# Four heads at a time: batching the heads of a gated linear attention in front of a cosine-gated MLP

## The chip, the cores and the metric

One NeuronCore of a Trainium2 chip runs the whole program. The time is what the device needs for one execution, in microseconds (us). Four timed runs of the kernel before gave 470.71 to 471.46 us with a median of 471.32. The profiled execution took 471.46 us.

The engines are named as in the profile: PE is TensorE's matmul, PEld its weight load, DVE is VectorE, ACT is ScalarE, POOL is GpSimd, SP is SyncE, which here only issues DMAs.

## The reference

The inputs q, k, v and f_logit have the shape (batch 4, heads 8, sequence 768, head size 48). For each batch and head a 48 x 48 state runs along the sequence; its rows decay by a gate, and the query reads it:

```python
f = 1.0 / (1.0 + np.exp(-f_logit))
for t in range(S):
    state = f[:, :, t, :, None] * state + np.einsum('bhd,bhe->bhde', k[:, :, t], v[:, :, t])
    y[:, :, t] = np.einsum('bhd,bhde->bhe', q[:, :, t], state)
```

The heads are then put side by side to a matrix x of 3072 tokens by 384, and an MLP with a cosine gate follows:

```python
h = x @ w_in            # 384 -> 2048
g = h * np.cos(h)
return g @ w_out        # 2048 -> 384
```

## The kernel before, in words

The program is written in a tile language: the code allocates tiles from pools, each tag (the tile's name) with its number of buffers, and a planner puts the instructions of each engine in one fixed order and adds the semaphores. Operations of `nc.any` go to VectorE or ScalarE as the planner chooses. Each engine runs its own list in order; a waiting instruction holds up those behind it. All DMAs are issued by SP, in one list.

**Constants (L38 to L54).** An identity, an upper triangular mask `umask` (128 x 128), and both weight matrices, which are loaded first (6 MB) and cast to bfloat16 on VectorE.

**Preparation of a head (L62 to L116).** For each of the 4 batches, `attn_batch` loops over the 8 heads. The sequence is cut into 6 chunks of 128 tokens; a tile has the 128 tokens of a chunk on its partitions and chunk by head size, 6 x 48 = 288 columns. Four DMAs of 144 KB bring q, k, v and f_logit. GpSimd casts v (`vc`). ScalarE takes Sigmoid and Ln of f_logit (L77, L79); the product of `umask` with the logarithms gives their running sum within each chunk (`pCum`), and two exponentials of it (L84, L86) give the decay `b_td` and its inverse. Six small matmuls give the sum over each whole chunk (`pBC`, L90), and `bC` (L93) is its exponential, the decay of the state over a chunk. Sigmoid, Ln and Exp each need a table in ScalarE; a change of table is an ACT_TABLE_LOAD in the profile. GpSimd zeroes `QK_td` and writes q times decay and k times inverse decay into it (L96 to L100). TensorE transposes it chunk by chunk (`pQK`, L104), and two copies bring `Qb_dt` and `Kb_dt` back to SBUF (L107, L109).

**Recurrence (L117 to L141).** Chunk by chunk, and within a chunk head by head, one unit of work is done:

- `pA` (L121) is the 128 x 128 product of keys and queries in the chunk; `Am` (L124) is pA times the mask.
- `pS` (L127) is the chunk's own contribution to the state.
- `pY` adds two matmuls: `vc` with `Am` (L130) and the state before the chunk with the queries (L131). `Yt` (L133) is its bfloat16 copy, and a DMA of 12 KB writes it to `xT` in DRAM (L135).
- `stmp` (L138) is pS plus the old state, and the new state (L140) is stmp times the decay of the chunk.

There are 4 x 6 x 8 = 192 units. `vc`, `bC`, `QK_td`, `Qb_dt` and `Kb_dt` have 9 buffers each; the other tiles of the preparation have 3, and those of the recurrence 6. In PSUM pCum, pBC, pS and pY have one buffer each, pQK and pA two.

**MoE stage (L143 to L164).** Six blocks of 512 tokens read `xT` back, multiply by w_in, take the cosine gate (ScalarE's Sin, VectorE's product) and multiply by w_out. It is not touched.

Of the kernel before, what the change touches and what calls it, by code (L numbers as in the profile page):

```python
# [9 lines left out]
F32 = mybir.dt.float32  # L10
BF16 = mybir.dt.bfloat16
AF = mybir.ActivationFunctionType
# [4 lines left out]
def kernel(  # L17
# [10 lines left out]
    nc = tc.nc  # L28
    B, H, S, D = q.shape
    C = 128  # L30
    NCH = S // C
# [9 lines left out]
    make_upper_triangular(nc, umask, val=1.0, diag=True)  # L41
    halfpi = cpool.tile([128, 1], F32, name="halfpi")
# [18 lines left out]

    def attn_batch(b, sb, sb2, stpool, ps, ps2):  # L62
        vc_l, bC_l, Qb_dt_l, Kb_dt_l, Kb_td_l, state_l = [], [], [], [], [], []
        for h in range(H):
            qh = sb.tile([C, NCH, D], F32, name="qh")
            kh = sb.tile([C, NCH, D], F32, name="kh")
            vh = sb.tile([C, NCH, D], F32, name="vh")
            fh = sb.tile([C, NCH, D], F32, name="fh")
# [3 lines left out]
            nc.sync.dma_start(out=fh, in_=f_logit[b, h].rearrange("(c p) d -> p c d", p=C))  # L72
            vc = sb.tile([C, NCH, D], BF16, name="vc", bufs=9)
            nc.gpsimd.tensor_copy(out=vc, in_=vh)

            sigf = sb.tile([C, NCH, D], F32, name="sigf")
            nc.scalar.activation(out=sigf, in_=fh, func=AF.Sigmoid)  # L77
            logf = sb.tile([C, NCH, D], BF16, name="logf")
            nc.scalar.activation(out=logf, in_=sigf, func=AF.Ln)  # L79
# [8 lines left out]
            pBC = ps.tile([D, NCH], F32, name="pBC", tag="pBC")  # L88
            for c in range(NCH):
                nc.tensor.matmul(pBC[:, c:c + 1], lhsT=logf[:, c, :],  # L90
                                 rhs=umask[:, C - 1:C], start=(c == 0), stop=(c == NCH - 1))
            bC = sb.tile([D, NCH], F32, name="bC", bufs=9)
            nc.scalar.activation(out=bC, in_=pBC, func=AF.Exp, scale=1.0)  # L93

            QK_td = sb.tile([C, NCH, C], BF16, name="QK_td", bufs=9)
# [10 lines left out]
            Qb_dt = sb.tile([D, NCH, C], BF16, name="Qb_dt", bufs=9)  # L106
            nc.any.tensor_copy(out=Qb_dt, in_=pQK[0:D])  # L107
            Kb_dt = sb.tile([D, NCH, C], BF16, name="Kb_dt", bufs=9)
            nc.any.tensor_copy(out=Kb_dt, in_=pQK[64:64 + D])  # L109

            state = stpool.tile([D, D], BF16, name="state")
            nc.gpsimd.memset(state, 0.0)
            vc_l.append(vc); bC_l.append(bC)
            Qb_dt_l.append(Qb_dt); Kb_dt_l.append(Kb_dt)
            Kb_td_l.append(Kb_td); state_l.append(state)
        for c in range(NCH):  # L116
            for h in range(H):  # L117
# [88 lines left out]
```

## Time and profile before

| | |
|---|---|
| median of 4 runs | 471.32 us |
| profiled execution | 471.46 us |
| its span (first to last instruction) | 469.7 us |
| busy in the span: PE / DVE / ACT / POOL | 337.8 / 229.3 / 314.7 / 85.0 us |
| DMA queue q1, share of 16 engines' span | 33.6% |
| attention, to the end of the last Yt | 333.7 us |
| MoE stage, from its first matmul to the end | 131.0 us |

Busy time of an engine is the time in which one of its instructions ran. Matmuls are pipelined, so their ends overlap with the next ones and a busy PE is not PE at its peak. In a row of the timeline the first number is the start in us from the span's start, the second the time in us; the brackets give the idle time of that engine just before, and what ended it. In a row of a group of instructions the shapes are partitions x elements, and after the bar stand busy time in us and the mean of one in ns, then idle time before.

### The profile page before, as it was taken

The page shows a single profiled execution, that of the slowest core. Times are in us where ns is not written, and L with a number is a line of the kernel's source. Part 1 is how long each engine was busy: PE and PEld are TensorE (multiplying, and loading weights), DVE is VectorE, ACT ScalarE, POOL GpSimd, SP SyncE. Part 2 cuts the span into 40 slices and gives each one's busy share as a digit, 9 for nine tenths or more (in the row PEclk, how much of TensorE's full clock was granted, in tenths as well). Part 3 has the DMA queues.
Part 4 walks back from the last instruction along what each step waited for, and adds up shares of the span by engine and source line. Part 5 has one row for each costly group of instructions (what it writes and reads, how often), then busy time and mean ns, then how long its engine had stood idle before and what let it go on. Part 6 is the DMA issues. An engine that isn't in the chain of part 4 may idle for free.

```text
span 469.7 us, 6528 instructions
## 1 busy us (share of the span) xinstructions
PE 337.8 (72%) x1850; PEld 175.6 (37%) x1856; DVE 229.3 (49%) x704; ACT 314.7 (67%) x606; POOL 85.0 (18%) x168
## 2 busy tenths in 40 slices
PE   0024448797769973344778876998399999999997
PEld 0012224344434431222434443443145455554544
DVE  0413336675535551233556563555073847557381
ACT  1099998988955665999999786555191825537180
POOL 6133221046210060322201723000000000000000
PEclk9999999999999999999999999999999999999999
DMA  8995563121521116955411224000302110100101
GB/s 326 296 153 117 101 114 64 36 49 34 97 47 27 26 36 108 147 107 105 82 34 39 47 48 83 13 14 13 113 29 85 50 69 17 51 34 35 52 17 67
DMA packets 120996, 35.04 MB, mean 75 GB/s; under 512 B 113152, under 2 KB 120576, under 8 KB 120576
## 3 DMA queue, kind: packets, MB, share of 16 engines
q1 hardware_dynamic: 120960, 34.63, 33.6%
q8 instruction: 14, 0.23, 0.2%
q14 instruction: 22, 0.18, 0.1%
HBM read 27.53 MB, written 7.08 MB: 74 GB/s over the span
## 4 chain that ended last, share of the span: by engine, by line
PE 53%; issue 14%; ACT 14%; DMA 6%; SPq 5%; POOL 4%; DVE 3%; ACTq 0%; DVEq 0%; POOLq 0%
PE ph L152 14%; PE po L160 13%; PE pY L130 7%; PE pY L131 6%; PE pA L121 5%; ACT L79 4%; PE pS L127 4%; SPq L69 2%; DMA vh<-in_v_dram 2%; PE pQK L104 2%; DMA fh<-in_f_logit_dram 2%; ACT Yt L133 2%; POOL QK_td L100 2%; ACT logf L79 1%; ACT L84 1%
## 5 line engine op out<-in xcount | busy, mean ns | idle before, releaser
L155 ACT ACTIVATE cosh<-ph,halfpi 128x512 bf16<-128x512 f32 x96 | 62.3, 687 | 52.8 <-PE ph L152 52.7
L124 DVE TENSOR_TENSOR Am<-pA,umask 128x128 bf16<-128x128 f32 x192 | 54.6, 290 | 40.4 <-PE pY L130 27.2
L156 DVE TENSOR_TENSOR gT<-ph,cosh 128x512 bf16<-128x512 f32 x96 | 62.4, 692 | 18.9 <-ACT cosh L155 18.9
L152 PE MATMUL ph<-xTt,w_in_bf 128*128 128x512 bf16 x282 | 65.6, 390 | 5.8 <-DMA xTt<-xT 5.3
L130 PE MATMUL pY<-Am,vc 128*48 128x128 bf16 x192 | 53.1, 276 | 21.1 <-ACT Yt L133 12.3
L121 PE MATMUL pA<-Qb_dt,Kb_dt 48*128 48x128 bf16 x192 | 51.3, 281 | 19.0 <-DVE Kb_dt L109 13.2
L160 PE MATMUL po<-w_out_bf,gT 128*128 128x384 bf16 x384 | 63.4, 326 | 0.0
L138 DVE TENSOR_TENSOR stmp<-pS,state 48x48 f32<-48x48 f32 x192 | 38.0, 198 | 44.3 <-PE pS L127 38.8
L131 PE MATMUL pY<-Qb_dt,state 48*48 48x128 bf16 x192 | 57.3, 298 | 0.0
L104 PE MATMUL pQK<-ident,QK_td 128*128 128x128 bf16 x192 | 27.9, 308 | 36.9 <-POOL QK_td L100 36.2
L133 ACT CAST Yt<-pY 48x128 bf16<-48x128 f32 x118 | 30.2, 256 | 35.7 <-PE pY L131 21.4
L140 ACT ACTIVATE state<-stmp,bC 48x48 bf16<-48x48 f32 x120 | 39.2, 332 | 15.4 <-DVE stmp L138 14.3
L127 PE MATMUL pS<-vc,QK_td 128*48 128x48 bf16 x192 | 43.4, 226 | 5.3 <-DVE stmp L138 2.6
L160 PEld LDWEIGHTS <-gT 128*128 128x128 bf16 x384 | 37.6, 98 | 25.5
L152 PEld LDWEIGHTS <-w_in_bf 128*128 128x128 bf16 x288 | 28.8, 100 | 41.0 <-issue 9.4
L107 DVE COPY Qb_dt<-pQK 48x768 bf16<-48x768 bf16 x26 | 14.3, 548 | 58.7 <-PE pQK L104 58.7
L77 ACT ACT_TABLE_LOAD x32 | 41.1, 1283 | 1.3 <-PEq L190 0.7
L131 PEld LDWEIGHTS <-state 48*48 48x48 bf16 x192 | 21.5, 112 | 54.2 <-issue 43.8
L82 PE MATMUL pCum<-logf,umask 128*128 128x288 bf16 x32 | 13.5, 422 | 39.3 <-ACT logf L79 39.3
L79 ACT ACT_TABLE_LOAD x32 | 41.1, 1283 | 0.6
L84 ACT ACT_TABLE_LOAD x30 | 38.5, 1283 | 0.9
L163 DVE COPY ot<-po 128x384 f32<-128x384 f32 x24 | 13.4, 558 | 43.9 <-PE po L160 43.9
(35 smaller groups left out, 336.0 us busy)
## 6 DMA issues: line engine op xcount, KB each, us to landing
qh<-in_q_dram SPq DMA_DIRECT2D x32, 144.0 KB, 2.6
kh<-in_k_dram SPq DMA_DIRECT2D x32, 144.0 KB, 3.0
vh<-in_v_dram SPq DMA_DIRECT2D x32, 144.0 KB, 3.4
fh<-in_f_logit_dram SPq DMA_DIRECT2D x32, 144.0 KB, 3.2
out_dram<-ot SPq DMA_DIRECT2D x24, 192.0 KB, 1.9
w_in_f<-in_moe_w_in_dram SPq DMA_DIRECT2D x1, 3072.0 KB, 9.9
w_out_f<-in_moe_w_out_dram SPq DMA_DIRECT2D x1, 3072.0 KB, 18.0
xT<-Yt SPq DMA_DIRECT2D x192, 12.0 KB, 1.4
```

Of the source, the lines that this page charges most:

```text
L77: nc.scalar.activation(out=sigf, in_=fh, func=AF.Sigmoid)
L79: nc.scalar.activation(out=logf, in_=sigf, func=AF.Ln)
L84: nc.scalar.activation(out=b_td, in_=pCum, func=AF.Exp, scale=1.0)
L121: nc.tensor.matmul(pA, lhsT=Kb_dt[:, c, :], rhs=Qb_dt[:, c, :], start=True, stop=True)
L124: nc.any.tensor_mul(out=Am, in0=pA, in1=umask)
L127: nc.tensor.matmul(pS, lhsT=Kb_td[:, c, :], rhs=vc[:, c, :], start=True, stop=True)
L130: nc.tensor.matmul(pY, lhsT=vc[:, c, :], rhs=Am, start=True, stop=False)
L131: nc.tensor.matmul(pY, lhsT=state, rhs=Qb_dt[:, c, :], start=False, stop=True)
L152: nc.tensor.matmul(ph, lhsT=w_in_bf[:, jk, jf * 128:(jf + 1) * 128], rhs=xTt[:, jk, :], start=(jk == 0), stop=(jk == KM - 1))
L155: nc.scalar.activation(out=cosh, in_=ph, func=AF.Sin, bias=halfpi)
L156: nc.vector.tensor_mul(out=gT[:, jf, :], in0=ph, in1=cosh)
L160: nc.tensor.matmul(po, lhsT=gT[:, jk, jt * 128:(jt + 1) * 128], rhs=w_out_bf[:, jk, :], start=(jk == 0), stop=(jk == KF - 1))
```

## The change

The heads are worked on in two groups of four.

- Sigmoid and Ln run once for four heads, on tiles of 128 x 4 x 288 (`fh4`, `sigf4`, `logf4`, 2 buffers each). The four f_logit loads of a group are issued ahead of the q, k and v loads of its first head.
- `pBC` is one PSUM tile for all 8 heads of a batch, and `bC` one exponential after the last head.
- `vc`, `QK_td`, `Qb_dt` and `Kb_dt` get 12 buffers for 9, bC has 3 for a batch each.
- A unit of the recurrence takes one chunk of four heads: the 16 matmuls are the same, but they write four neighbouring slices of one PSUM tile, and Am, Yt, stmp, the new state and the DMA to xT are one instruction each. `umask_g` holds the mask four times for Am. The new state was a product with one scalar per partition; it is now a product of two tensors, with bC broadcast along 48 columns. Yt is bound to VectorE.
- In PSUM pA has one buffer for two and pY two for one.

```diff
...
+    HG_ = 4
+    umask_g = cpool.tile([128, HG_, 128], BF16, name="umask_g")
+    for _i in range(HG_):
+        make_upper_triangular(nc, umask_g[:, _i, :], val=1.0, diag=True)
...
+    HG = 4
+    NG = H // HG
+
     def attn_batch(b, sb, sb2, stpool, ps, ps2):
-        vc_l, bC_l, Qb_dt_l, Kb_dt_l, Kb_td_l, state_l = [], [], [], [], [], []
+        vc_l, Qb_dt_l, Kb_dt_l, Kb_td_l = [], [], [], []
+        pBC = ps.tile([D, H, NCH], F32, name="pBC", tag="pBC")
         for h in range(H):
+            if h % 4 == 0:
+                fh4 = sb.tile([C, 4, NCH, D], F32, name="fh4", bufs=2)
+                for i in range(4):
+                    nc.sync.dma_start(out=fh4[:, i], in_=f_logit[b, h + i].rearrange("(c p) d -> p c d", p=C))
+                sigf4 = sb.tile([C, 4, NCH, D], F32, name="sigf4", bufs=2)
+                nc.scalar.activation(out=sigf4, in_=fh4, func=AF.Sigmoid)
+                logf4 = sb.tile([C, 4, NCH, D], BF16, name="logf4", bufs=2)
+                nc.scalar.activation(out=logf4, in_=sigf4, func=AF.Ln)
+            logf = logf4[:, h % 4]
             qh = sb.tile([C, NCH, D], F32, name="qh")
             kh = sb.tile([C, NCH, D], F32, name="kh")
             vh = sb.tile([C, NCH, D], F32, name="vh")
-            fh = sb.tile([C, NCH, D], F32, name="fh")
...
-            nc.sync.dma_start(out=fh, in_=f_logit[b, h].rearrange("(c p) d -> p c d", p=C))
-            vc = sb.tile([C, NCH, D], BF16, name="vc", bufs=9)
+            vc = sb.tile([C, NCH, D], BF16, name="vc", bufs=12)
             nc.gpsimd.tensor_copy(out=vc, in_=vh)
 
-            sigf = sb.tile([C, NCH, D], F32, name="sigf")
-            nc.scalar.activation(out=sigf, in_=fh, func=AF.Sigmoid)
-            logf = sb.tile([C, NCH, D], BF16, name="logf")
-            nc.scalar.activation(out=logf, in_=sigf, func=AF.Ln)
 
...
-            pBC = ps.tile([D, NCH], F32, name="pBC", tag="pBC")
             for c in range(NCH):
-                nc.tensor.matmul(pBC[:, c:c + 1], lhsT=logf[:, c, :],
-                                 rhs=umask[:, C - 1:C], start=(c == 0), stop=(c == NCH - 1))
-            bC = sb.tile([D, NCH], F32, name="bC", bufs=9)
-            nc.scalar.activation(out=bC, in_=pBC, func=AF.Exp, scale=1.0)
-
-            QK_td = sb.tile([C, NCH, C], BF16, name="QK_td", bufs=9)
+                nc.tensor.matmul(pBC[:, h, c:c + 1], lhsT=logf[:, c, :],
+                                 rhs=umask[:, C - 1:C], start=(h == 0 and c == 0),
+                                 stop=(h == H - 1 and c == NCH - 1))
+
+            QK_td = sb.tile([C, NCH, C], BF16, name="QK_td", bufs=12)
...
-            Qb_dt = sb.tile([D, NCH, C], BF16, name="Qb_dt", bufs=9)
+            Qb_dt = sb.tile([D, NCH, C], BF16, name="Qb_dt", bufs=12)
             nc.any.tensor_copy(out=Qb_dt, in_=pQK[0:D])
-            Kb_dt = sb.tile([D, NCH, C], BF16, name="Kb_dt", bufs=9)
+            Kb_dt = sb.tile([D, NCH, C], BF16, name="Kb_dt", bufs=12)
...
-            state = stpool.tile([D, D], BF16, name="state")
+            vc_l.append(vc)
+            Qb_dt_l.append(Qb_dt); Kb_dt_l.append(Kb_dt)
+            Kb_td_l.append(Kb_td)
+        bC = sb.tile([D, H, NCH], F32, name="bC", bufs=3)
+        nc.scalar.activation(out=bC, in_=pBC, func=AF.Exp, scale=1.0)
+
+        state_l = []
+        for g in range(NG):
+            state = stpool.tile([D, HG, D], BF16, name="state")
             nc.gpsimd.memset(state, 0.0)
-            vc_l.append(vc); bC_l.append(bC)
-            Qb_dt_l.append(Qb_dt); Kb_dt_l.append(Kb_dt)
-            Kb_td_l.append(Kb_td); state_l.append(state)
+            state_l.append(state)
         for c in range(NCH):
-            for h in range(H):
-                vc = vc_l[h]; bC = bC_l[h]; Qb_dt = Qb_dt_l[h]
-                Kb_dt = Kb_dt_l[h]; Kb_td = Kb_td_l[h]; state = state_l[h]
-                pA = ps2.tile([C, C], F32, name="pA", tag="pA", bufs=2)
-                nc.tensor.matmul(pA, lhsT=Kb_dt[:, c, :], rhs=Qb_dt[:, c, :],
-                                 start=True, stop=True)
-                Am = sb2.tile([C, C], BF16, name="Am")
-                nc.any.tensor_mul(out=Am, in0=pA, in1=umask)
-
-                pS = ps2.tile([D, D], F32, name="pS", tag="pS")
-                nc.tensor.matmul(pS, lhsT=Kb_td[:, c, :], rhs=vc[:, c, :],
-                                 start=True, stop=True)
-                pY = ps2.tile([D, C], F32, name="pY", tag="pY")
-                nc.tensor.matmul(pY, lhsT=vc[:, c, :], rhs=Am, start=True, stop=False)
-                nc.tensor.matmul(pY, lhsT=state, rhs=Qb_dt[:, c, :], start=False, stop=True)
-                Yt = sb2.tile([D, C], BF16, name="Yt")
-                nc.any.tensor_copy(out=Yt, in_=pY)
-                tok0 = b * S + c * C
-                nc.sync.dma_start(out=xT[h * D:(h + 1) * D, tok0:tok0 + C], in_=Yt)
-
-                stmp = sb2.tile([D, D], F32, name="stmp")
+            tok0 = b * S + c * C
+            for g in range(NG):
+                h0 = g * HG
+                state = state_l[g]
+                pA = ps2.tile([C, HG, C], F32, name="pA", tag="pA", bufs=1)
+                for i in range(HG):
+                    nc.tensor.matmul(pA[:, i, :], lhsT=Kb_dt_l[h0 + i][:, c, :],
+                                     rhs=Qb_dt_l[h0 + i][:, c, :],
+                                     start=(i == 0), stop=(i == HG - 1))
+                Am = sb2.tile([C, HG, C], BF16, name="Am")
+                nc.any.tensor_mul(out=Am, in0=pA, in1=umask_g)
+
+                pS = ps2.tile([D, HG, D], F32, name="pS", tag="pS")
+                for i in range(HG):
+                    nc.tensor.matmul(pS[:, i, :], lhsT=Kb_td_l[h0 + i][:, c, :],
+                                     rhs=vc_l[h0 + i][:, c, :],
+                                     start=(i == 0), stop=(i == HG - 1))
+                pY = ps2.tile([D, HG, C], F32, name="pY", tag="pY", bufs=2)
+                for i in range(HG):
+                    nc.tensor.matmul(pY[:, i, :], lhsT=vc_l[h0 + i][:, c, :],
+                                     rhs=Am[:, i, :], start=(i == 0), stop=False)
+                for i in range(HG):
+                    nc.tensor.matmul(pY[:, i, :], lhsT=state[:, i, :],
+                                     rhs=Qb_dt_l[h0 + i][:, c, :],
+                                     start=False, stop=(i == HG - 1))
+                Yt = sb2.tile([D, HG, C], BF16, name="Yt")
+                nc.vector.tensor_copy(out=Yt, in_=pY)
+                nc.sync.dma_start(
+                    out=xT[h0 * D:(h0 + HG) * D, tok0:tok0 + C].rearrange(
+                        "(hl p) t -> p hl t", p=D),
+                    in_=Yt)
+
+                stmp = sb2.tile([D, HG, D], F32, name="stmp")
                 nc.any.tensor_add(out=stmp, in0=pS, in1=state)
-                newstate = stpool.tile([D, D], BF16, name="state")
-                nc.any.tensor_scalar_mul(out=newstate, in0=stmp, scalar1=bC[:, c:c + 1])
-                state_l[h] = newstate
+                newstate = stpool.tile([D, HG, D], BF16, name="state")
+                bC_s = bC[:, h0:h0 + HG, c:c + 1].broadcast_to([D, HG, D])
+                nc.any.tensor_mul(out=newstate, in0=stmp, in1=bC_s)
+                state_l[g] = newstate
```

## Rows read from the trace of the kernel before

**Rows 1.** the page, busy us of each engine (share of the span) and instructions

```profile
PE 337.8 (72%) x1850; PEld 175.6 (37%) x1856; DVE 229.3 (49%) x704; ACT 314.7 (67%) x606; POOL 85.0 (18%) x168
```

**Rows 2.** windows: busy us of each engine (instructions), PEclk, DMA share, GB/s

```profile
22.40:70.90 48.50, 18.26 (x142) 10.93 (x142) 15.81 (x47) 47.73 (x70) 14.97 (x25) 1.00 0.72 124
70.90:137.00 66.10, 52.68 (x290) 27.60 (x291) 38.21 (x160) 55.06 (x111) 20.48 (x39) 1.00 0.28 51
137.00:173.00 36.00, 32.03 (x157) 15.20 (x156) 20.55 (x91) 22.68 (x70) 6.81 (x17) 1.00 0.19 37
173.00:227.00 54.00, 20.67 (x146) 11.79 (x145) 15.01 (x45) 46.77 (x73) 14.45 (x24) 1.00 0.62 108
```

**Rows 3.** timeline, the last Yt

```profile
333.42 0.26 ACT L133 CAST Yt<-pY 48x128 bf16<-48x128 f32 x1 [0.58 <-PE pY L131]
```

**Rows 4.** groups by line and form, preparation

```profile
L77 ACT ACT_TABLE_LOAD x32 | 41.1, 1283 | 1.3 <-PEq L190 0.7
...
L79 ACT ACT_TABLE_LOAD x32 | 41.1, 1283 | 0.6
...
L84 ACT ACT_TABLE_LOAD x30 | 38.5, 1283 | 0.9
...
L99 POOL TENSOR_TENSOR QK_td<-qh,b_td 128x288 bf16<-128x288 f32 x32 | 23.3, 728 | 61.6 <-ACT b_td L84 53.8 <-issue 3.8 <-DMA qh<-in_q_dram 3.5
...
L96 POOL MEMSET QK_td<- 128x768 bf16 x32 | 23.3, 738 | 56.5 <-PE pS L127 56.2
...
L74 POOL CAST vc<-vh 128x288 bf16<-128x288 f32 x32 | 14.4, 451 | 72.6 <-DMA vh<-in_v_dram 44.5 <-PE pA L121 21.0 <-PE pY L130 7.0
```

**Rows 5.** timeline, first preparation, two pA one after the other

```profile
59.95 0.28 PE L121 MATMUL pA<-Qb_dt,Kb_dt 48*128 48x128 bf16 x1 [0.95 <-DVE Kb_dt L109]
...
65.52 0.29 PE L121 MATMUL pA<-Qb_dt,Kb_dt 48*128 48x128 bf16 x1 [0.96 <-DVE Kb_dt L109]
```

**Rows 6.** timeline, recurrence of batch 1, two Yt one after the other

```profile
159.25 0.26 ACT L133 CAST Yt<-pY 48x128 bf16<-48x128 f32 x1
...
160.14 0.26 ACT L133 CAST Yt<-pY 48x128 bf16<-48x128 f32 x1
```

**Rows 7.** waits: who waited for whom, us in total, times, longest

```profile
POOL QK_td L96 <- PE pS L127: 56.2, 6, 22.1
```

**Rows 8.** timeline, ScalarE at the start of batch 0

```profile
22.42 0.44 ACT L77 ACTIVATE sigf<-fh 128x288 f32<-128x288 f32 x1 [20.39 <-DMA fh<-in_f_logit_dram]
...
22.88 1.28 ACT L79 ACT_TABLE_LOAD   x1
...
24.17 0.44 ACT L79 ACTIVATE logf<-sigf 128x288 bf16<-128x288 f32 x1
```

**Rows 9.** groups by line and form, VectorE and ScalarE

```profile
L124 DVE TENSOR_TENSOR Am<-pA,umask 128x128 bf16<-128x128 f32 x192 | 54.6, 290 | 40.4 <-PE pY L130 27.2 <-PE pA L121 11.4
...
L156 DVE TENSOR_TENSOR gT<-ph,cosh 128x512 bf16<-128x512 f32 x96 | 62.4, 692 | 18.9 <-ACT cosh L155 18.9
...
L138 DVE TENSOR_TENSOR stmp<-pS,state 48x48 f32<-48x48 f32 x192 | 38.0, 198 | 44.3 <-PE pS L127 38.8 <-PE pY L130 1.4 <-ACT state L140 1.0
...
L133 DVE CAST Yt<-pY 48x128 bf16<-48x128 f32 x74 | 20.7, 280 | 14.2 <-PE pY L131 12.4 <-DMA vh<-in_v_dram 1.6
...
L109 DVE COPY Kb_dt<-pQK 48x768 bf16<-48x768 bf16 x25 | 14.0, 559 | 0.8
...
L109 ACT COPY Kb_dt<-pQK 48x768 bf16<-48x768 bf16 x7 | 5.6, 795 | 0.2
```

**Rows 10.** timeline, six transposes of one head

```profile
63.10 0.82 PE L104 MATMUL pQK<-ident,QK_td 128*128 128x128 bf16 x6 [2.00 <-POOL QK_td L100]
```

**Rows 11.** timeline and line L140: a state update beside GpSimd

```profile
166.32 2.97 POOL L96 MEMSET QK_td<- 128x768 bf16 x4 [0.36 <-PE pS L127]
...
167.89 0.72 DVE L140 TENSOR_SCALAR state<-stmp,bC 48x48 bf16<-48x48 f32 x1
...
L140 DVE TENSOR_SCALAR state<-stmp,bC x72: 228/234/745, 32.1 to 293.7; 48x48 bf16<-48x48 f32 x72
```

## The prediction

> **What bounds the kernel now.** Read the page's engine line first [rows 1]: no engine is busy for more than 72% of the span, so the average names no bound and the stages have to be taken apart. The windows do that [rows 2]. From 22.4 to 70.9 us the heads of batch 0 are prepared, and ScalarE is busy 47.7 of 48.5 us. From 70.9 to 137 the recurrence of batch 0 and the preparation of batch 1 share the time. From 137 to 173 the recurrence of batch 1 runs almost alone and no engine is full. From 173 to 227 batch 2 is prepared, with ScalarE at 46.8 of 54 us. Batches 2 and 3 repeat batches 0 and 1, and the MoE stage starts after the last head [rows 3].
>
> In the preparation ScalarE is held by table loads: 32, 32 and 30 of 1.28 us on the sigmoid, logarithm and exponential lines, 120.7 us [rows 4]. One head costs three of them, and successive heads are 5.57 us apart [rows 5]. In the recurrence alone, one unit (a chunk of one head) follows the one before by 0.89 us [rows 6]; VectorE and ScalarE are busy for under two thirds of that window, so this is a chain through the single pY buffer (second pY matmul, Yt, the next unit's first pY), not a full engine.
>
> Two facts set how the stages overlap. First, in the preparation there is one pA per 5.57 us [rows 5]: head 0 could have gone on to chunk 1 but didn't. Tiles of one tag are handed out in program order, and the next unit in that order belongs to a head that isn't ready. Second, GpSimd's zeroing of QK_td waited 56.2 us in 6 waits on pS [rows 7]: the next batch's heads wait until the old recurrence gives their buffers back. With 9 buffers and 8 heads, one head runs ahead.
>
> **The change part by part.** Durations are of the profiled execution (471.46 us; span 469.7 and 1.76 around it; the runs' median of 471.32 is 0.14 lower).
>
> *Table loads.* Sigmoid and Ln run once per four heads. Their tiles are 128x1152. From 0.44 us at 288 columns [rows 8] and 0.795 at 768 [rows 9] ScalarE takes 0.74 ns a column, so 1.1 us each (at least 0.44, at most four times that, 1.77). If each group of four needs one load for each function, 24 loads remain: some 70 go, 90 us of ScalarE, most of which lay on the path of the two preparation windows. The row says 1.28 us for a load, and the activation after it starts 0.01 us later [rows 8]. The Trainium skill (ScalarE: Activation LUTs, What ACT_TABLE_LOAD costs) adds a drain and budgets about 2.66 us for a switch; by that the five switches left in batch 0's preparation would cost 6.9 us more and the sum below would be 344. The trace disagrees: load and activation follow with no drain between them.
>
> *Preparation of batch 0.* The four f loads take the place of the first head's four, so the first sigmoid stays at 22.4 us [rows 8]. Sigmoid 1.1, load 1.28, Ln 1.1, load 1.28: the first exponential is at 27.2. Per head ScalarE then needs two exponentials, at most the sigmoid's 0.44 each, with a matmul between heads (estimate 0.4, half the transposes' 0.82 [rows 10]), 1.3; GpSimd needs two products of 0.73 and the cast of 0.45, 1.9 [rows 4]. Group 1 follows after three more loads and 2.2 us of sigmoid and Ln, near 38.4 us; its four products end near 47, then transposes 0.82 and two copies of 0.56 [rows 9]. The loads of eight heads bring the same: 124 GB/s at 0.72 share [rows 2] is 172 GB/s if full, 0.59 MB a head in 3.4 us, 27 us for eight, behind the weights. I put the last head at 50 us instead of 70.9. The four extra masks and the longer zeroing (12 tiles) lie on GpSimd while it waits for data, at nothing; uncovered, twelve zeroings of 0.74 cost 9 us.
>
> *The new unit.* Four heads go together: 48 units instead of 192. On VectorE a unit has Am on 512 columns, 0.69 (the gT row is the same shape); Yt on 512, 0.28 + 384 x 1.05 ns = 0.68; stmp on 192, 0.20 + 0.15 = 0.35 [rows 9]. The new state is now a product of two SBUF tensors with a broadcast, which no row shows: at least stmp's 0.20, at most 0.35 plus one GpSimd product of 0.73 in front of it; I take 0.35, as stmp has its size. The sum is 2.07 us. TensorE has 16 matmuls at no more than the 0.1 of a transpose (0.82 for six, the last with its full latency [rows 10]): 1.6, beside it. pA now has one buffer, so the next pA waits for this Am, and on TensorE pS, pY and preparation matmuls queue behind it. If pY and Yt come before the next Am, the cycle is 0.69 + 0.8 + 0.15 + 0.68 = 2.3; else 2.07. I take 2.3. Four old units are 3.6.
>
> newstate also waits for bC, which now needs all eight heads; behind it on VectorE stand Am and Yt of group 1, and the next batch's copies. That wait hides behind group 1's own wait for its heads, since bC needs their Ln but not their products; uncovered it costs the 2 us of chunk 0. Yt is bound to VectorE; the transfers to xT are 48 for 192, so loads queued behind them on SP wait on fewer. The batched state zeroing and bC are off the path.
>
> *Overlap.* With 12 buffers, four heads of the next batch are prepared during a recurrence. The other four wait for the last chunk of group 0, some 3.2 us before its end. Program order holds as before: chunk 0 of group 1 is the second unit, so nothing beyond one unit runs ahead. GpSimd then needs 4 x (0.45 + 0.74 + 1.46) = 10.6, and transposes and copies 2.2: 12.8, a gap of 9.6 behind the old recurrence. The kernel before did worse than its buffers: 66.1 - 36 = 30 us for seven heads [rows 2], 17.1 for four. I take the middle, 13.4.
>
> *Sum.* A recurrence after the gap is 11 units of 2.3 and about 2.5 of next-batch copies on VectorE, 28. Last Yt: 50 + 28 + 3 x (13.4 + 28) - 2.5 = 199.7, against 333.7 [rows 3]. From there to the end 136.0 us are untouched code. 335.7 + 1.76 = **337 us**. Unit times of 2.07 and 2.6 move it by -10 and +13, gaps of 9.6 and 17.1 by 11 either way: 315 to 362 for this case.
>
> **The rivals.**
> - *No gap.* The instruction order lets everything but VectorE hide: 50 + 4 x 28 - 2.5 = 159.5, **297**. For it: twelve buffers, a GpSimd preparation of 21 us a batch. Against: one pA per head [rows 5].
> - *Whole batches in series*, as in the 54 us window [rows 2]: preparation instructions stand ahead of the last units in the in-order queues. Eight heads of 2.65 and 9 of ends are 30 a gap, 3 x 16.6 more: **387**.
> - *newstate behind GpSimd.* The old state update on VectorE took 0.72 us where its median is 0.23, while GpSimd zeroed buffers [rows 11]. If each new one waits for a product, 48 x 0.73 = 35 come on VectorE's path: **372**. The Trainium skill (SBUF — State Buffer, Who interferes with whom) has it so: a VectorE instruction with two SBUF inputs waits for a GpSimd instruction that reads SBUF until that ends. No row before has such a product. GpSimd has reading work for only four heads during a recurrence, 7.6 of 28 us, so most should go free.
> - *The loads stay.* If the order alternates sigmoid, Ln and exponentials of two groups head by head, a head keeps 5.57: first recurrence 19 us later, gaps 8 longer: **381**.
> - *Slower.* The unit turns into one serial chain through the single pA and pS. The last Yt is 97.7 + 44 units' time, so it is slower from 5.4 us a unit. Matmuls 0.7 and 1.0, VectorE 2.07, a product of 0.73 in the way and six hand-overs of 0.1 are 5.1; another 0.3 and the time is **473**. Against: four VectorE operations of two groups have nothing in common but buffers.
>
> **How the numbers follow.** Forecast 0.64, no gap 0.12, series 0.12, newstate 0.06, loads 0.04, slower 0.02. The range 300 to 385 leaves out half of no gap (0.06), two thirds of series and a third of loads, since these sizes spread by 10 or more (0.09), and slower (0.02): 0.17. A measurement here tells 0.2% from no change. Faster by more has 0.97, within it 0.01, slower 0.02.
>
> **What would show it.** Right: some 24 to 34 table loads; first chunk of group 1 near 50 us; units 2.1 to 2.5 apart with VectorE nearly full; three stretches of 10 to 17 us in which VectorE thins out and GpSimd is full; last Yt near 200; 136 us behind it. Wrong: loads still near 98, units above 3 us, state products well above 0.35, or gaps of 30 us with the matmuls of one batch waiting on GpSimd products of the next.

## The result and the profile after

The changed kernel takes 364.88 us (median of 8 runs, 364.40 to 365.54) against 470.69 (13 runs, 470.05 to 471.46): a ratio of 0.7753, 95% interval 0.7744 to 0.7761. The forecast of 337 us had the direction and lay 28 us too low; the time is inside the range of 300 to 385, which was widened for the rivals, but outside the 315 to 362 that the prediction worked out for its own case. The profiled run took 364.62 us, with a span of 362.8.

The engine line of the page after, which answers to [rows 1]:

```profile
PE 267.9 (74%) x1850; PEld 160.8 (44%) x1856; DVE 186.5 (51%) x332; ACT 171.6 (47%) x252; POOL 83.7 (23%) x152
```

ScalarE lost most of its table loads. The groups of its lines (busy us, mean ns; then idle time ahead and what ended it), in place of [rows 4]:

```profile
L78 ACT ACT_TABLE_LOAD x8 | 10.3, 1283 | 31.8 <-DMA fh<-in_f_logit_dram 31.7
L80 ACT ACT_TABLE_LOAD x8 | 10.3, 1283 | 0.1
L95 ACT ACT_TABLE_LOAD x8 | 10.3, 1283 | 17.9 <-PE pCum L93 17.9
L78 ACT ACTIVATE sigf<-fh 128x1152 f32<-128x1152 f32 x8 | 9.3, 1162 | 1.5 <-DMA fh<-in_f_logit_dram 1.4
```

24 loads, as forecast, and 1.16 us for an activation of four heads (forecast 1.1). The first line already holds the news: ScalarE waited 31.7 us for f, 22.6 of them at the start of the kernel and the rest in front of later groups.

Where the span goes is read from the windows (busy us of PE, PEld, DVE, ACT, POOL; clock, DMA share, GB/s). I cut at the last pA of the first unit of group 1 (within half a us), and at the last Yt of each batch, so that preparation, recurrence and gap follow one another:

```profile
22.40:54.80 32.40, 15.84 (x132) 10.03 (x131) 6.75 (x14) 25.62 (x38) 14.44 (x24) 1.00 1.03 155
54.80:86.50 31.70, 26.91 (x225) 18.24 (x226) 21.70 (x45) 14.86 (x21) 13.14 (x22) 1.00 0.43 83
86.50:103.40 16.90, 8.50 (x71) 5.38 (x70) 4.07 (x8) 12.86 (x20) 7.22 (x12) 1.00 0.88 152
103.40:136.80 33.40, 26.76 (x225) 18.25 (x226) 20.98 (x44) 14.77 (x21) 12.97 (x22) 1.00 0.40 78
136.80:154.10 17.30, 8.12 (x67) 5.10 (x67) 3.93 (x8) 12.54 (x19) 7.23 (x12) 1.00 0.90 157
154.10:186.00 31.90, 26.84 (x229) 18.46 (x229) 21.69 (x47) 16.02 (x22) 10.38 (x18) 1.00 0.42 82
186.00:201.90 15.90, 8.11 (x67) 5.10 (x67) 4.00 (x8) 11.29 (x18) 7.16 (x12) 1.00 0.73 119
201.90:230.20 28.30, 20.99 (x169) 14.10 (x168) 20.56 (x43) 0.24 (x1) 0.00 (x0) 1.00 0.10 18
230.20:362.80 132.60, 125.82 (x666) 66.00 (x672) 75.56 (x121) 63.40 (x97) 0.00 (x0) 1.00 0.16 55
```

| term | forecast | measured | difference |
|---|---|---|---|
| first unit of group 1 | 50.0 | 54.8 | +4.8 |
| four recurrences | 109.5 | 125.3 | +15.8 |
| three gaps | 40.2 | 50.1 | +9.9 |
| last Yt to the end | 136.0 | 132.6 | -3.4 |
| span | 335.7 | 362.8 | +27.1 |

In a gap VectorE is busy for 4 of 17 us, GpSimd for 7, and DMA for 0.73 to 0.90 of the time; in the three recurrences beside which a batch is prepared VectorE is busy for 21 to 22 of 32 us and DMA for 0.40 to 0.43 of the time. The timeline of one unit, VectorE and TensorE:

```profile
57.02 0.68 DVE L158 CAST Yt<-pY 48x512 bf16<-48x512 f32 x1 [0.27 <-PE pY L154]
...
57.62 0.67 DVE L142 TENSOR_TENSOR Am<-pA,umask_g 128x512 bf16<-128x512 f32 x1
...
58.22 0.34 DVE L165 TENSOR_TENSOR stmp<-pS,state 48x192 f32<-48x192 f32 x1
58.35 0.58 PE L151 MATMUL pY<-Am,vc 128*48 128x128 bf16 x4 [0.55 <-DVE Am L142]
...
58.60 0.35 DVE L168 TENSOR_TENSOR state<-stmp,bC 48x192 bf16<-48x192 f32 x1
58.87 0.62 PE L154 MATMUL pY<-Qb_dt,state 48*48 48x128 bf16 x4
59.42 0.60 PE L138 MATMUL pA<-Qb_dt,Kb_dt 48*128 48x128 bf16 x4
59.52 0.68 DVE L158 CAST Yt<-pY 48x512 bf16<-48x512 f32 x1 [0.57 <-PE pY L154]
...
60.13 0.67 DVE L142 TENSOR_TENSOR Am<-pA,umask_g 128x512 bf16<-128x512 f32 x1
```

A unit takes 2.51 us (57.62 to 60.13). Am runs, then eight pY matmuls from 58.35 to 59.49, then Yt and the next Am. VectorE stands idle for 0.57 in each. The next pA comes after both halves of pY in TensorE's order, and that decides the first experiments below.

The gap between batch 0 and batch 1, SyncE, ScalarE and GpSimd (SPq rows are the issue of a transfer):

```profile
75.89 0.33 SPq L159 DMA_DIRECT2D xT<-Yt  x1
76.31 0.40 SPq L76 DMA_DIRECT2D fh<-in_f_logit_dram  x1
...
78.40 0.33 SPq L159 DMA_DIRECT2D xT<-Yt  x1
78.78 1.02 SPq L76 DMA_DIRECT2D fh<-in_f_logit_dram  x2
...
81.48 0.33 SPq L159 DMA_DIRECT2D xT<-Yt  x1
81.85 0.45 SPq L76 DMA_DIRECT2D fh<-in_f_logit_dram  x1
...
86.05 1.28 ACT L78 ACT_TABLE_LOAD   x1 [4.76 <-DMA fh<-in_f_logit_dram]
...
92.81 0.41 ACT L95 ACTIVATE b_td<-pCum 128x288 bf16<-128x288 f32 x1
93.35 0.73 POOL L108 TENSOR_TENSOR QK_td<-qh,b_td 128x288 bf16<-128x288 f32 x1 [3.12 <-DMA kh<-in_k_dram]
...
102.92 0.80 ACT L118 COPY Kb_dt<-pQK 48x768 bf16<-48x768 bf16 x1
103.78 0.28 PE L138 MATMUL pA<-Qb_dt,Kb_dt 48*128 48x128 bf16 x1 [0.79 <-ACT Kb_dt L118]
```

The last Yt of batch 0 ends at 86.5. The f loads of group 1 were issued one or two at a time, each behind a transfer to xT that waits for its Yt. So ScalarE has f only at 86.05; the first exponential is at 92.81, four heads of products follow, and the last head's Kb_dt is copied at 102.92. SyncE's own queue says the same: transfers to xT wait for a Yt 43 times, 95.5 us in all, the longest 8.2.

```profile
SPq L159 <- DVE Yt L158: 95.5, 43, 8.2
```

### The profile page after: what moved, and what is told of

It is laid out like the page before. It is cut to its first block, busy times and chain, and to the rows that moved or that the text cites. A ratio compares the mean times of both kernels' runs of the same rounds, so it can differ in the third digit from the quotient of the medians.

```text
span 362.8 us, 5159 instructions
## 1 busy us (share of the span) xinstructions
PE 267.9 (74%) x1850; PEld 160.8 (44%) x1856; DVE 186.5 (51%) x332; ACT 171.6 (47%) x252; POOL 83.7 (23%) x152
## 4 chain that ended last, share of the span: by engine, by line
PE 54%; ACT 11%; DVE 9%; issue 8%; DMA 6%; POOL 6%; SPq 5%; POOLq 0%; ACTq 0%
PE po L188 17%; PE ph L180 16%; PE pY L151 6%; PE pY L154 6%; DVE Yt L158 4%; SPq L76 4%; DVE Am L142 4%; PE pQK L113 4%; DMA fh<-in_f_logit_dram 3%; POOL QK_td L109 3%; ACT L95 2%; PE pA L138 2%; POOL QK_td L108 2%; PE pCum L93 2%; ACT L80 1%
## 5 line engine op out<-in xcount | busy, mean ns | idle before, releaser
L158 DVE CAST Yt<-pY 48x512 bf16<-48x512 f32 x48 | 32.8, 683 | 39.7 <-PE pY L154 39.1
L93 PE MATMUL pCum<-logf,umask 128*128 128x288 bf16 x32 | 13.4, 419 | 46.6 <-ACT logf L80 39.5
L151 PE MATMUL pY<-Am,vc 128*48 128x128 bf16 x192 | 28.5, 303 | 20.0 <-DVE Am L142 20.0
L116 ACT COPY Qb_dt<-pQK 48x768 bf16<-48x768 bf16 x28 | 22.2, 791 | 32.9 <-PE pQK L113 32.9
L191 DVE COPY ot<-po 128x384 f32<-128x384 f32 x24 | 13.4, 558 | 43.9 <-PE po L188 43.9
L138 PE MATMUL pA<-Qb_dt,Kb_dt 48*128 48x128 bf16 x192 | 31.7, 302 | 4.1 <-ACT Kb_dt L118 4.1
L151 PEld LDWEIGHTS <-vc 128*48 128x48 bf16 x192 | 20.7, 141 | 28.8 <-issue 28.6
L142 DVE TENSOR_TENSOR Am<-pA,umask_g 128x512 bf16<-128x512 f32 x48 | 32.4, 674 | 1.5 <-PE pA L138 1.5
L108 POOL TENSOR_TENSOR QK_td<-qh,b_td 128x288 bf16<-128x288 f32 x32 | 23.3, 729 | 41.7 <-ACT b_td L95 36.1
L168 DVE TENSOR_TENSOR state<-stmp,bC 48x192 bf16<-48x192 f32 x48 | 19.0, 397 | 20.8 <-ACT bC L124 19.5
L154 PE MATMUL pY<-Qb_dt,state 48*48 48x128 bf16 x192 | 29.7, 308 | 0.0
L113 PEld LDWEIGHTS <-QK_td 128*128 128x128 bf16 x192 | 18.0, 138 | 25.0 <-POOL QK_td L109 24.2
L100 PEld LDWEIGHTS <-logf 128*48 128x48 bf16 x192 | 8.5, 130 | 40.2 <-issue 40.2
L78 ACT ACT_TABLE_LOAD x8 | 10.3, 1283 | 31.8 <-DMA fh<-in_f_logit_dram 31.7
```

Source lines behind the costliest of these rows:

```text
L108: nc.gpsimd.tensor_mul(out=Qb_td, in0=qh, in1=b_td)
L113: nc.tensor.matmul(pQK[:, c, :], lhsT=QK_td[:, c, :], rhs=ident, is_transpose=True, start=(c == 0), stop=(c == NCH - 1))
L138: nc.tensor.matmul(pA[:, i, :], lhsT=Kb_dt_l[h0 + i][:, c, :], rhs=Qb_dt_l[h0 + i][:, c, :], start=(i == 0), stop=(i == HG - 1))
L142: nc.any.tensor_mul(out=Am, in0=pA, in1=umask_g)
L151: nc.tensor.matmul(pY[:, i, :], lhsT=vc_l[h0 + i][:, c, :], rhs=Am[:, i, :], start=(i == 0), stop=False)
L154: nc.tensor.matmul(pY[:, i, :], lhsT=state[:, i, :], rhs=Qb_dt_l[h0 + i][:, c, :], start=False, stop=(i == HG - 1))
```

## The experiments

The sums below are read from the rows of Yt in each trace: *start* is the second Yt of batch 0 (chunk 0 of group 1); *R* adds, over the four batches, the time from the second Yt to the last; *G* adds the three times from a batch's last Yt to the second Yt of the next batch. Start + R + G is the start of the last Yt. The column *us* is the profiled run's time.

| kernel | us | start | R | G |
|---|---|---|---|---|
| changed kernel | 364.62 | 57.0 | 112.6 | 59.9 |
| f loads early | 360.39 | 58.2 | 112.2 | 54.7 |
| 16 buffers | 364.72 | 56.9 | 112.6 | 59.8 |
| Yt on ScalarE | 371.56 | 57.1 | 105.8 | 73.1 |
| two pA, one pQK | 373.25 | 60.8 | 96.8 | 79.3 |
| Yt and xT issue on ScalarE | 360.76 | 57.4 | 103.0 | 65.1 |
| two pA, one pY | 363.25 | 57.1 | 99.9 | 70.2 |
| units alone | 394.47 | 73.5 | 125.8 | 56.4 |
| early f, two pA, one pY | 353.78 | 58.5 | 94.2 | 65.6 |
| the same, xT issue on ScalarE | 337.74 | 58.5 | 92.3 | 51.1 |
| the same, 16 buffers | 333.78 | 58.5 | 92.5 | 47.6 |
| the same, copies on VectorE | 333.86 | 55.9 | 90.8 | 51.3 |

All but the first and the last are single runs. The 8 runs of the changed kernel lie within 1.1 us and the 13 of the kernel before within 1.4, so smaller differences tell nothing.

**1. The f loads of both groups at the start of a batch.**

```diff
+        fh4_l = []
+        for g in range(NG):
+            fh4 = sb.tile([C, 4, NCH, D], F32, name="fh4", bufs=4)
+            for i in range(4):
+                nc.sync.dma_start(out=fh4[:, i], in_=f_logit[b, 4 * g + i]...)
+            fh4_l.append(fh4)
```

> The f_logit loads of both groups are issued at the start of a batch (fh4 with 4 buffers); nothing else changes. Theory A: the 16 to 17 us between a batch's last Yt and the next batch's first pA of group 1 are set by the f loads of group 1, which stand late in SP's list behind transfers to xT. Then the gap falls to the 9.6 us that buffers and GpSimd would leave, three times 7, and the time to about 345 us. Rival B: the gap is set by the buffers that come back at the end of the recurrence and by GpSimd's 10.6 us behind that. Then nothing moves: 363 to 367 us.

360.39 us, 4.2 less: a part of what was expected. ScalarE no longer waits for f in the gap, but what comes next is late as well. The timeline of the last heads in the gap between batches 0 and 1:

```profile
95.01 0.82 PE L117 MATMUL pQK<-ident,QK_td 128*128 128x128 bf16 x6
95.86 0.79 ACT L120 COPY Qb_dt<-pQK 48x768 bf16<-48x768 bf16 x1 [1.13 <-PE pQK L117]
96.69 0.80 ACT L122 COPY Kb_dt<-pQK 48x768 bf16<-48x768 bf16 x1
...
97.54 0.28 PE L142 MATMUL pA<-Qb_dt,Kb_dt 48*128 48x128 bf16 x1 [1.55 <-ACT Kb_dt L122]
97.75 0.82 PE L117 MATMUL pQK<-ident,QK_td 128*128 128x128 bf16 x6
```

A head is a chain of 2.75 us: its transposes, two copies on ScalarE, its pA matmul, and only then in TensorE's order the transposes of the next head. This is slower than the 1.9 us that GpSimd needs per head. So in the last heads of the gap this chain comes behind the loads. The q, k and v loads are still issued behind the transfers to xT here; experiment 10 takes those out of the way.

**2. 16 buffers for 12** (sigmoid in place, to make room).

```diff
-            vc = sb.tile([C, NCH, D], BF16, name="vc", bufs=12)
+            vc = sb.tile([C, NCH, D], BF16, name="vc", bufs=16)
...
```

(QK_td, Qb_dt and Kb_dt likewise.)

> 16 buffers for 12 in vc, QK_td, Qb_dt and Kb_dt, so that all eight heads of the next batch have buffers (Sigmoid works in place to make room). Theory A (late f loads): the gaps stay at 16 to 17 us, 362 to 367 us. Rival B (buffers and GpSimd): group 1 is prepared during the recurrence, gaps of 4 us or less, 325 to 330 us.

364.72 us, no change in any column. The buffers, on which the prediction based its shortest gap, don't bound the changed kernel: the next batch's data comes later than they do.

**3. Yt on ScalarE.**

```diff
-                nc.vector.tensor_copy(out=Yt, in_=pY)
+                nc.scalar.copy(out=Yt, in_=pY)
```

> Yt is copied by ScalarE instead of VectorE. Theory A: a unit of 2.51 us is the chain Am, the two groups of pY matmuls, Yt, next Am, because VectorE's list has Yt ahead of the next Am. Then a unit falls to TensorE's own 2.0 to 2.1 us, 44 units save 18 us: about 347 us. Rival B: TensorE's order (pA of the next unit behind pY of this one) sets the cycle with Am in it: 0.67 + 1.14 + pA 0.6 + hand-overs 0.1 are 2.5 too, and nothing moves: 362 to 367 us.

371.56 us. The rows of Am show whether VectorE's order of Yt before Am made the unit:

```profile
106.51 0.69 DVE L142 TENSOR_TENSOR Am<-pA,umask_g 128x512 bf16<-128x512 f32 x1 [0.18 <-PE pA L138]
...
108.97 0.69 DVE L142 TENSOR_TENSOR Am<-pA,umask_g 128x512 bf16<-128x512 f32 x1 [0.85 <-PE pA L138]
```

With Yt gone from VectorE, units are still 2.46 apart, and now Am waits for pA. So the theory that VectorE's order sets the unit fell, and TensorE's order (rival B) is left, which experiments 4 and 6 try: the next pA needs the one pA buffer, stands behind this unit's pY, and that waits for this Am. The unit runs round Am, pY, pA. The time is above both expectations: the gaps grew by 13 us, with the f loads of the next batch later still (the sigmoid of group 1 of batch 1 starts at 91.05 instead of 87.34).

**4. Two pA buffers** and one of pQK.

```diff
-                pA = ps2.tile([C, HG, C], F32, name="pA", tag="pA", bufs=1)
+                pA = ps2.tile([C, HG, C], F32, name="pA", tag="pA", bufs=2)
-            pQK = ps.tile([C, NCH, C], BF16, name="pQK", tag="pQK", bufs=2)
+            pQK = ps.tile([C, NCH, C], BF16, name="pQK", tag="pQK")
```

> pA gets two PSUM buffers and pQK one. Theory A: VectorE's order sets the unit, and pA's buffer doesn't count: units stay at 2.5 us, and the single pQK buffer costs up to 1 us a head in the gaps, 365 to 380 us. Rival B: with a second buffer pA of the next unit goes ahead of pY of this one, units of 2.1 us, 18 us less: 347 to 358 us.

373.25 us: the units of rival B, in the time of theory A. Where nothing runs beside them (batch 3) units come in pairs of 4.04 us, and R falls by 15.8, which confirms the single pA. But G grows by 19.4 and start by 3.8; experiment 6, with pQK in two buffers again, has 9.1 and 3.7 less.

**5. Yt and the issue of its transfer on ScalarE**, so that SyncE holds loads alone.

```diff
-                nc.sync.dma_start(
+                nc.scalar.dma_start(
                     out=xT[h0 * D:(h0 + HG) * D, tok0:tok0 + C]...
```

(and the edit of experiment 3)

> Yt is copied by ScalarE as in e3_yt_act (371.6 us, units 2.46), and the transfers to xT are issued by ScalarE too, so SP's list holds nothing but loads. Theory A: the gaps (about 20 us in e3) come from loads that stand behind transfers to xT, which wait for their Yt. Then q, k, v and f of the next batch arrive during the recurrence, gaps of 10 to 12 us, about 342 to 350 us. Rival B: the loads come late because the planner places them late or their own buffers are not free, whatever shares the list: gaps stay near 20 us and the time near 371.

360.76 us, 10.8 less than experiment 3, from which it differs in the queue of the transfers alone; this is between the two expectations. G is 8.0 less, R 2.8. But 10.8 is a net figure: the three gaps were 24.4 each in experiment 3 and are 37.7, 7.7 and 19.6 here. So the gaps behind batches 1 and 2 are shorter, and the one behind batch 0 is 13.3 longer. That ScalarE now stands behind the transfers that it issues is the likely reason for it; experiment 10 shows a row of this.

**6. Two pA buffers and one of pY** (pQK keeps two).

```diff
-                pA = ps2.tile([C, HG, C], F32, name="pA", tag="pA", bufs=1)
+                pA = ps2.tile([C, HG, C], F32, name="pA", tag="pA", bufs=2)
-                pY = ps2.tile([D, HG, C], F32, name="pY", tag="pY", bufs=2)
+                pY = ps2.tile([D, HG, C], F32, name="pY", tag="pY")
```

> pA gets two PSUM buffers, pY one; pQK keeps its two. Theory A: the unit of 2.51 us is the chain Am, pY, pA of the next unit on TensorE, next Am, because the single pA buffer puts that pA behind this pY (e4 with two pA gave 2.02 us a unit and lost it in the gaps). Then units of 2.0 to 2.1 us, 44 x 0.45 = 20 us less in the recurrences; gaps of 17 us unchanged: 345 us. Rival B: a single pY puts Yt into the chain (1.1 + 0.7 + hand-overs, 2.0), so the same 2.0 to 2.1, or if pY waits for Yt of the unit before in the wrong order, 2.5 as now: 365.

363.25 us: the unit of both expectations, and nearly the 365 of rival B, which expected it with units of 2.5. The unit fell to 1.91 us, shown by two Yt and the pY between them:

```profile
61.06 0.68 DVE L158 CAST Yt<-pY 48x512 bf16<-48x512 f32 x1 [0.36 <-PE pY L154]
...
61.80 0.58 PE L151 MATMUL pY<-Am,vc 128*48 128x128 bf16 x4 [0.23 <-DVE Yt L158]
...
62.31 0.62 PE L154 MATMUL pY<-Qb_dt,state 48*48 48x128 bf16 x4
...
62.97 0.68 DVE L158 CAST Yt<-pY 48x512 bf16<-48x512 f32 x1 [0.36 <-PE pY L154]
```

This is the ring that rival B named: pY waits for the one pY buffer until Yt has read it, and the next Yt waits for pY. VectorE is idle for 0.36 in it. A full VectorE would come to the same pace: by the starts of the unit shown above, Yt takes 0.60 until Am can start, Am 0.60, stmp 0.38, the new state 0.35, 1.93 in all. Late in batch 3 (Yt from 215.69 to 223.37) units are 1.92 apart with VectorE idle for only 0.1 in each, so there the two bounds meet. What a second pY would give with two pA and two pQK wasn't tried.

R fell by 12.7, and 10.3 came back in G. By batches it is plainer: the recurrences of batches 0 to 2 lost 6.9 us, less than their gaps gained, since f came later (the same sigmoid at 90.06 instead of 87.34). What was won is batch 3, which has no gap behind it: 25.1 to 19.3.

**7. The units alone**: four heads a unit and 12 buffers, with Sigmoid and Ln per head.

```diff
-                fh4 = sb.tile([C, 4, NCH, D], F32, name="fh4", bufs=2)
...
+            sigf = sb.tile([C, NCH, D], F32, name="sigf")
+            nc.scalar.activation(out=sigf, in_=fh, func=AF.Sigmoid)
+            logf = sb.tile([C, NCH, D], BF16, name="logf")
+            nc.scalar.activation(out=logf, in_=sigf, func=AF.Ln)
```

> The changed kernel with Sigmoid and Ln per head, as before the change: the grouped units, the buffers and the rest stay. Three table loads a head are back (about 96). Prediction's split: the loads are worth the ScalarE pace of 5.57 us a head where the preparation is on the path: 16 to 19 us in batch 0 and 8 to 12 in each gap, 45 to 55 together: 410 to 420 us. Rival: the gaps are set by late transfers anyway, and only batch 0 loses: 380 to 390 us.

**8. The loads alone**: the kernel before with Sigmoid and Ln over four heads.

```diff
+            if h % 4 == 0:
+                fh4 = sb.tile([C, 4, NCH, D], F32, name="fh4", bufs=2)
...
+                nc.scalar.activation(out=logf4, in_=sigf4, func=AF.Ln)
+            logf = logf4[:, h % 4]
```

> The kernel before with nothing but Sigmoid and Ln taken over four heads (24 or so loads for 98); units of one head, 9 buffers. Prediction's split: preparation of batches 0 and 2 falls from 48 and 54 us to about 30, batches 1 and 3 little: 471 - 45 = 425 us. Rival: with 9 buffers and units in program order the preparation of a batch stays serial behind GpSimd and transfers, and only batch 0 gains: 445 to 455 us.

394.47 and 460.48 us, neither on its expectation. Of the 106 us, units and buffers alone bring 77 and the batched functions alone 11; together they bring 18 more than the sum. With units, batching is worth 29.6 (start 16.5, R 13.3 and the tail behind the last Yt 3.6, while G is 3.5 longer). Without them, heads that are ready early seem to run into the buffers (argued, as no run had more of them there): GpSimd's zeroing waits for the old recurrence 90.4 us, where before it was 56.2 [rows 7].

```profile
POOL QK_td L98 <- PE pS L129: 90.4, 3, 30.3
```

**9. Early f loads with two pA and one pY** (the edits of 1 and 6).

```diff
+            fh4 = sb.tile([C, 4, NCH, D], F32, name="fh4", bufs=4)
...
+                pA = ps2.tile([C, HG, C], F32, name="pA", tag="pA", bufs=2)
+                pY = ps2.tile([D, HG, C], F32, name="pY", tag="pY")
```

> f loads of both groups at the start of a batch's preparation, and pA in two buffers (pY in one). Theory A, the loads of the next batch stand behind the xT transfers on SyncE and arrive at the recurrence's pace, whatever the units take: units near 1.9 us, but a gap that grows by what the recurrence loses, so within 4 us of the early f loads alone (360.4), 357 to 362. Theory B, with f early the rest of the gap is the chain of heads (2.75 us a head), which doesn't depend on the loads: the gap stays near 15 us and four recurrences of some 5 us less give about 342.

353.78 us: nearer to theory A, but under its interval. Against experiment 1, R is 18.0 less and G 11.0 more. In batches 0 to 2 this is theory A: R lost 12.3, and the gaps behind took back 11.0. The other 5.6 are the recurrence of batch 3, which has no gap behind it and which the interval of theory A had left out. Theory B's gap near 15 us did not come (21.6 to 22.1).

**10. The same with the xT transfers issued by ScalarE** (Yt stays on VectorE).

```diff
-                nc.sync.dma_start(
+                nc.scalar.dma_start(
                     out=xT[h0 * D:(h0 + HG) * D, tok0:tok0 + C]...
```

> As the run before it in this list, with the xT transfers issued by ScalarE instead of SyncE (Yt stays on VectorE), so that SyncE holds loads alone. Theory A (transfers in front of the loads set the gap): loads of the next batch issue during the recurrence, gap down to the 10 to 12 us that GpSimd and the copies of four heads need, 325 to 335. Theory B (chain of heads sets it): like the run before it within 5 us. Rival C: ScalarE now waits for Yt in front of each transfer and its copies come late; slower than the run before it.

337.74 us, 16.0 less, 14.5 of it in G. Transfers in front of loads on one queue are the largest single cost of the gaps that a run here priced. It stops 3 us above theory A's interval: by the rows of Yt two gaps fell from 22 to 13.9 and 11.8, but the one behind batch 0 grew from 21.9 to 25.4. Rival C shows up there: the Ln of batch 1 stood 5 us behind transfers to xT on ScalarE, each of which waits for its Yt.

```profile
61.42 2.22 ACTq L163 DMA_DIRECT2D xT<-Yt  x2
63.67 1.28 ACT L84 ACT_TABLE_LOAD   x1 [5.00 <-DVE Yt L162]
```

**11. The same with 16 buffers**, as in experiment 2 (sigmoid in place; here the tiles of the recurrence have 4 buffers for 6 and the state 12 for 18, to make room).

```diff
+            vc = sb.tile([C, NCH, D], BF16, name="vc", bufs=16)
...
```

> As the run before it in this list, with 16 buffers instead of 12 for vc, QK_td, Qb_dt and Kb_dt (sigmoid in place, fewer Yt and state buffers to make room). Theory A, buffers are the next limit once the loads come early: all eight heads of the next batch can be prepared during a recurrence, gaps under 6 us, 305 to 318. Rival, the order of the instructions on TensorE (pA of the next unit stands before the pQK of the next head) is the limit and not the buffers: within 3 us of the run before it.

333.78 us, 4.0 less: a little more than the rival allowed. Buffers count once the loads come early, but not by the 20 us or more of theory A.

**12. The same with both copies of a head on VectorE.**

```diff
-            nc.any.tensor_copy(out=Qb_dt, in_=pQK[0:D])
+            nc.vector.tensor_copy(out=Qb_dt, in_=pQK[0:D])
-            nc.any.tensor_copy(out=Kb_dt, in_=pQK[64:64 + D])
+            nc.vector.tensor_copy(out=Kb_dt, in_=pQK[64:64 + D])
```

> As the version with early f loads, pA in two buffers, transfers issued by ScalarE and 16 buffers (333.8 us), with both copies of a head (Qb_dt and Kb_dt) bound to VectorE, 0.55 us each instead of 0.79 on ScalarE. Theory A, the last heads of a preparation run as a chain, pQK 0.82, Qb, Kb, pA, then the next head's pQK, 2.75 us a head: the last heads come 2.25 us apart, the first chunk of group 1 of batch 0 is masked near 54.5 us instead of 56.6, each gap loses some 2 us, and the time is 325 to 328. Rival B, VectorE fills up in the recurrences: 31 more copies there are 17 us, about 4 a batch, and the time is 338 to 350. If both are worth the same, 331 to 336.

333.17 us (median of 4, 332.92 to 333.86), a ratio to the kernel before of 0.7072, interval 0.7060 to 0.7084. The chain is confirmed where it was forecast; the last heads of batch 0:

```profile
50.79 0.56 DVE L121 COPY Kb_dt<-pQK 48x768 bf16<-48x768 bf16 x1
...
53.05 0.56 DVE L121 COPY Kb_dt<-pQK 48x768 bf16<-48x768 bf16 x1
```

2.25 us apart, and the start moves from 58.5 to 55.9. The first gap falls by 5.5 as well, from 25.4, but the two later ones grow by 9.1, so in sum the two are worth the same. Experiments 11 and 12 are the fastest versions, 8.5% and 8.7% below the changed kernel. In experiment 12 the Ln of batch 1 still waits 5.2 us on ScalarE behind transfers to xT. What else holds the first gap (19.9 us of G) stays open, and so does what an issuer other than SyncE and ScalarE would give: none was tried.

## Why the prediction was right, and where it was off

The mechanisms held in the main: loads off ScalarE, four heads to a unit, four heads of the next batch prepared in a gap. The time lies in the range because the range was made wide for the rivals; it is 3 us above what the forecast's own case allowed. Two of the signs of being right did not come: VectorE is not nearly full in a unit (idle for 0.57 of 2.51 us), and GpSimd is not full in the gaps (7.2 of 16.9 us). Of the 27.1 us of span that were missing, the terms that were mis-sized are these.

**The new unit, 2.3 us; measured 2.51.** The price of VectorE was right but for the overlap of successive instructions: 2.07 forecast, 1.93 by starts. The cycle was chosen as the bound and is it, but its pY was put at 0.8 and takes 1.14 us for the eight matmuls, 0.14 each where the forecast took 0.1 at most from the transposes [rows 10]. 44 units by 0.21 are 9.2 of the 15.8 us in the recurrences. The condition "if pY and Yt come before the next Am" named Yt; experiments 3, 4 and 6 put pA in its place.

**The copies of the next batch, 2.5 us a recurrence.** The recurrence of batch 3, with nothing beside it, takes 28.3; the three others 31.7, 33.4 and 31.9, so 3.4 to 5.1, 12.1 in sum against the forecast's 7.5. It isn't VectorE that is short but TensorE: between the Yt at 64.54 and the one at 69.59, two units' time, it ran 24 pBC, two pCum and the pQK of a head in front of a pY whose Am was done at 65.82:

```profile
66.51 0.82 PE L113 MATMUL pQK<-ident,QK_td 128*128 128x128 bf16 x6 [0.49 <-POOL QK_td L109]
67.26 0.84 PE L100 MATMUL pBC<-umask,logf 128*48 128x1 bf16 x17
...
68.39 0.62 PE L151 MATMUL pY<-Am,vc 128*48 128x128 bf16 x4
```

The rest of the difference in the recurrences, 2 us, is the last Yt of each, less a rounding.

**The gap, 13.4 us; measured 16.9, 17.3 and 15.9.** The step that failed is the one that built the gap from buffers and GpSimd (9.6) and took the middle towards the old 17.1. Experiment 2 shows that buffers don't count here. What stands in the gap is a chain the sum left out, from 86.05 to 92.81: table load, sigmoid, table load, Ln, cumulative sum, table load, 6.8 us. It is there because the f loads queue behind the transfers to xT. The prediction had named that queue and let it off, since 48 transfers for 192 mean fewer waits; but SyncE issues in order, and a load behind a transfer waits for that transfer's Yt, however few the transfers are. Moving the transfers to ScalarE gained 10.8 us in experiment 5 and 16.0 in experiment 10, net of what ScalarE lost by it.

**The first preparation, 50 us; measured 54.8.** Two things were missing. The sigmoid's table load stood at 0.74 in the trace before, ahead of the data; now it waits for the data and the first exponential is at 28.83 instead of 27.2:

```profile
22.59 1.28 ACT L78 ACT_TABLE_LOAD   x1 [22.59 <-DMA fh<-in_f_logit_dram]
23.88 1.16 ACT L78 ACTIVATE sigf<-fh 128x1152 f32<-128x1152 f32 x1
25.06 1.28 ACT L80 ACT_TABLE_LOAD   x1
26.36 1.16 ACT L80 ACTIVATE logf<-sigf 128x1152 bf16<-128x1152 f32 x1
```

And group 1's sigmoid follows the copies of group 0's last head on ScalarE, at 39.70. Experiment 1 shows that undoing this alone is worth nothing: the Ln of group 1 came at 33.3 instead of 42.2 and the start came 1.2 later, not earlier, because then the chain of 2.75 us a head is last, which experiment 12 shortened.

**The tail, 136.0 us; measured 132.6.** Taken as untouched. The MoE's first loads of xT are now issued at 229.67, beside the last Yt, and its first matmul is 2.8 us behind the end of that Yt where it was 5.05. With the units alone or the loads alone (experiments 7 and 8) it is 5.4, so this needs both parts of the change; why stays open. The other 1.2 us lie in the MoE stage itself, 131.0 before and 129.8 now.

**The rivals.** *Whole batches in series* wanted gaps of 30, *the loads stay* some 90 loads, *slower* units of 5.4; none came. *No gap* (297) isn't the changed kernel, though the last versions go about half of the way from 364.9 to it. *newstate behind GpSimd* is real and small: the new state has a mean of 397 ns over 48, and where one starts beside a GpSimd product it lasts longer, up to 0.84 us:

```profile
76.67 0.73 POOL L108 TENSOR_TENSOR QK_td<-qh,b_td 128x288 bf16<-128x288 f32 x1
76.76 0.84 DVE L168 TENSOR_TENSOR state<-stmp,bC 48x192 bf16<-48x192 f32 x1
```

Against 0.35 for a free one that is 48 by 0.05, 2.3 us instead of 35. The Trainium skill (SBUF — State Buffer, Who interferes with whom), by which a VectorE instruction with two SBUF inputs contends with a GpSimd instruction that reads SBUF, is borne out in such rows. The prediction's reason for a low chance, that GpSimd has little work during a recurrence, was the right one: 34 of the 48 met no GpSimd instruction and took 0.34 or 0.35.

The Trainium skill (ScalarE: Activation LUTs, What ACT_TABLE_LOAD costs) budgets 2.66 us for a switch; the rows at 22.59 to 26.36 show a load of 1.28 and load and activation following each other within 0.02, so no drain, and the trace disagrees with it as before.

## What to carry to other kernels

Batching instructions removes what stands in the recurrence, but the time shows up as gaps until the loads of the next batch stop queueing behind the stores of this one: give loads and dependent stores different queues before shortening the work between them, and look at what then stands behind the stores (on ScalarE a Ln waited 5 us for them). Where a buffer is cut to one, look at the order of the engine that fills it, and not only at the engine that frees it. A stage's price must hold the whole chain from its loads, function tables included, and not only the engine that is busiest in it.

## What was not expected of the hardware

- Behind Yt and Am, which the rows give 0.68 and 0.67, the next VectorE instruction starts after 0.60: a sum of such durations is 0.07 or 0.08 too large for each. Behind stmp it isn't so where the new state, which reads it, is next (0.34, the next after 0.38); late in batch 3 of experiment 6, where the next one is an Am, it is (0.34, the next after 0.27).
- The two copies out of one pQK never ran side by side on two engines: with Qb_dt on VectorE and Kb_dt on ScalarE the second began when the first ended (the row of Kb_dt at 37.60 waited 0.70 for Qb_dt, which ran from 37.02 for 0.55). Whether the chip or the program orders them wasn't tried.
